# Attention and two-layer MLP on one core: early quotients through two other DMA queues, two runs of scores for the first four pairs, a later scaling, a new table of shifts

## The chip, the cores and the metric

The kernel runs on one core of a Trainium2 chip. The metric is the device time of one execution in microseconds (us), the median of several runs. A core has a TensorE (PE, with PEld for its weight loads), a VectorE (DVE), a ScalarE (ACT), a GpSimd (POOL) and a SyncE (SP). SP, ACT and POOL can each issue DMA transfers; a DMA instruction stands in the order of the engine that issues it, and whatever it has to wait for holds up what stands behind it on that engine.

## The reference, cut

```python
# q, k, v: (8, 8, 576, 64)   f: (8, 8, 576) in 0.8..1   w_in: (512, 2048)   w_out: (2048, 512)
scores = matmul(q, k.T) / 8
cum    = cumsum(log(clip(f, 1e-4, 1)))              # along the sequence
scores = where(causal, -1e9, scores + cum[:, None] - cum[None, :])
attn   = exp(scores - max);  attn = attn / (sum(attn) + 1e-9)
x      = matmul(attn, v) -> (4608, 512)             # tokens x (heads * 64)
h      = x @ w_in;  g = max(h, 0) + alpha * min(h, 0);  out = g @ w_out
```

All in float32.

## The kernel before

**The parts.** Heads go in pairs, `attention(n)` for n = 0 to 31; pairs 4b to 4b+3 make the rows of batch b. A pair has its scores in four row tiles (widths 128, 256, 384, 512) per head and one tail tile for the last 64 rows of both heads. For each tile PE multiplies q and k (L381, `bank<-rqk`), DVE adds the mask and decay `Z` and takes the row minimum in one instruction (L830, the tail at L680), ACT takes the exponential with the row sum into `st` (L637), PE transposes the tile (L651), DVE (pairs 0 to 3, even widths) or ACT copies it out of the bank (L646, L647), and PE multiplies it with v (L381, `bank<-big,vr`). ACT copies the values to `xs` (L925).

**Quotients.** When a pair has all sums, ACT adds eps (L726), DVE takes the reciprocal (L727), PE transposes the 128x9 result (L729), ACT copies it to `R` (L730), and then the row of 576 quotients per head has to reach all partitions: SP stores `R` to DRAM (L735, `rd<-R`) and SP loads it back three times, spread over 64 partitions each (`fetch`, L742, `ri<-rd`). There is one buffer `ri`. The values are multiplied with it (L939, two instructions a pair: DVE for n < 8, POOL later), and ACT and POOL split the product into the two parts that the MLP takes (L941, L943, into `xx`). Pair 3 (`hurry`) does without DRAM: `quick` spreads its quotients by PE products. From pair 6 on, two pairs share one store (`mate`), so there are five stores of 9x128 and one of 18x128 for n < 8, and seven groups of three fetches.

**Masks.** f is loaded, clipped, its logarithm taken and summed (`cu`, L403). DVE scales it by -8 (`o_8`, L408), SP stores it (`c8`, L410) and a second form of it (`c8p`), and each pair's `Z` is loaded from there, spread over partitions (L533, L575), before POOL adds the triangle (L557, L558, L577). The first pair's mask is made by PE products and DVE (L550).

**Between.** w_in comes in 16 chunks, each loaded by SP (L362) and split by DVE (L367, L368, L371, L372), ACT and POOL. The first MLP layer (`bank<-xx,wi`) starts as soon as batch 0 is there and from then on fills PE wherever attention leaves it idle; its results go to DRAM, and the second layer runs from about 500 us.

**The order.** Nothing is ordered by hand. `Plan` holds all operations with an engine, an assumed cost, the data and buffers they need, and a key; it walks through time, gives each engine the operation that can start earliest and, among these, the one with the smallest key. To the key it adds `SHIFT[(kind, pair)]`, a table of some 280 numbers (kinds are loads L, masks D and Z, scores A, transposes T, values V, quotients Q, multiplies X, splits W). Each engine then runs its instructions in the planned order. The order of scores of the first four pairs comes from `stretch`, once for each set of tiles in L953. Where the plan sees PE idle for over 0.5 us before 82 us, `fill` (L476) writes matmuls of `ident` with itself into the order; they compute nothing.

Of the kernel before, what the change touches and what calls it, by code (L numbers as in the profile page):

```python
# [13 lines left out]
AF = mybir.ActivationFunctionType  # L14
# [3 lines left out]
B, H, S, D = 8, 8, 576, 64  # L18
# [85 lines left out]
class Plan:  # L104
# [36 lines left out]
    def run(self):  # L141
# [7 lines left out]
        while left:  # L149
# [41 lines left out]
            if o.kb:  # L191
                self.chan = max(self.chan, s + 1.4) + o.kb / (220.0 if s < FAR else 280.0)
                end = self.chan + 1.0
# [29 lines left out]
def attention_moe(  # L223
# [110 lines left out]
    def c_act(n):  # L334
        return 65 + n / 1.2
# [53 lines left out]
    o_w1 = op("POOL", 100, lambda: po.memset(warm, 1.0), -102)  # L389
    o_w2 = op("ACT", 1400, lambda: ac.activation(warm, warm, AF.Ln), -102, [o_w1])  # L390
    o_f = op("SP", 500, lambda: sy.dma_start(ft(), f.rearrange("b h s -> (b h) s")), -100, (), [bft], kb=144)
    o_z = op("DVE", 500, lambda: ve.memset(z(), 0.0), -100, (), [bz])

    o_clip, o_ln, o_sc = [], [], []
    PC = ((0, 256), (256, S))
    for a0, a1 in PC:
        o_clip.append(op("DVE", 130 + (a1 - a0), lambda a0=a0, a1=a1: ve.tensor_scalar(
            ft()[:, a0:a1], ft()[:, a0:a1], 1e-4, 1.0, ALU.max, ALU.min), -100, [o_f], [bft]))
    for i, (a0, a1) in enumerate(PC):
        o_ln.append(op("ACT", c_act(a1 - a0) + 180, lambda a0=a0, a1=a1: ac.activation(ft()[:, a0:a1], ft()[:, a0:a1], AF.Ln), -100, [o_clip[i]], [bft]))  # L400
    o_warm = op("ACT", 1500, lambda: ac.activation(warm, ft()[0:1, 0:1], AF.Exp), -99, o_ln, [bft])
    for i, (a0, a1) in enumerate(PC):
        o_sc.append(op("DVE", 100 + 2.2 * (a1 - a0), lambda i=i, a0=a0, a1=a1: ve.tensor_tensor_scan(  # L403
            cu()[:, a0:a1], ft()[:, a0:a1], z()[:, a0:a1], cu()[:, a0 - 1 : a0] if i else 0.0, ALU.add, ALU.add),
            -100, [o_ln[i], o_z] + o_sc, [bft, bz, bcu]))
    o_scan = o_sc[1]

    o_8 = [op("DVE", 150 + (a1 - a0) / 1.92, lambda a0=a0, a1=a1: ve.tensor_scalar_mul(ft()[:, a0:a1], cu()[:, a0:a1], -8.0),  # L408
              -100, [o_sc[i]], [bcu, bft]) for i, (a0, a1) in enumerate(PC)]
    o_c8 = op("SP", 400, lambda: sy.dma_start(c8, ft()), -49, o_8, [bft], kb=147)  # L410
    o_c8p = [op("SP", 400, lambda k=k: sy.dma_start(c8p[:, 128 * k : 128 * k + 128].rearrange("p (s c) -> p s c", c=32),
                                                    c8[:, 0:512].rearrange("p (s k c) -> p s k c", k=4, c=32)[:, :, k]), 6, [o_c8], kb=60) for k in range(4)]
    o_c8p.append(op("SP", 400, lambda: sy.dma_start(c8p[:, 512:S], c8[:, 512:S]), 6, [o_c8], kb=16))
# [67 lines left out]
    first_up = []
    x_ops, x_late, xt_ops, s_0 = {}, [], [], []

    def load_n(n, held):

        b, p = divmod(n, NP)
        first = n == 0
        kl, kc, bh = NS * n - 16, NS * n - 7, b * H + 2 * p
        bqk, bZ = Buf(rqk), Buf(rZ)
        q_, k_ = (lambda: bqk.t[:, 0:QW]), (lambda: bqk.t[:, QW : QW + S])  # L490
        plan.at("L", n)
        kq = -99 if first else -59 if n == 1 else kl
        dq = [] if first else [o_scan]
# [23 lines left out]
        for h in range(2):  # L517
# [876 lines left out]
```

## Time and profile before

| | |
|---|---|
| median of 3 runs | 991.21 us (990.93 to 991.32) |
| the profiled execution | 990.63 us, its span 988.8 us |
| busy share of the span | PE 99%, DVE 84%, ACT 62%, POOL 38% |
| granted TensorE clock | 1.00 of full speed (2.4 GHz) in all stretches |
| first MLP product | at 59.01 us |

The span is what the trace covers; the rest of the time lies around it. A stretch is read by its busy times: an engine whose busy time is as long as the stretch sets its end. The chain of waits goes back from the last instruction, at each step to what released it. "Idle before" is the time an engine stood still just ahead of an instruction, with what it waited for.

### The profile page before, as it was taken

To read this page: it belongs to the slowest core of one execution; us is meant where nothing else is said; L and a number is where in the kernel's file an instruction comes from. 1 tells how busy PE (TensorE), PEld (TensorE's weight loads), DVE (VectorE), ACT (ScalarE), POOL (GpSimd) and SP (SyncE) were. 2 spreads that over 40 slices of the span, in tenths; PEclk is the share of its full clock that TensorE was granted. 3 is DMA by queue.
4 is the path that set the end of the run, shared out by engine and by line. 5 is a ranking of instruction groups with operands and counts; after the bars stand their busy time and mean duration, and the time that the engine had idled before them with its cause. 6 is when DMAs were issued, how large, how long until landed. Compare 5 with 4: busy or idle time off the path is not lost.

```text
span 988.8 us, 20133 instructions
## 1 busy us (share of the span) xinstructions
PE 982.2 (99%) x6935; PEld 827.5 (84%) x6935; DVE 830.7 (84%) x1585; ACT 614.4 (62%) x1399; POOL 375.5 (38%) x652
## 2 busy tenths in 40 slices
PE   9999999999999999999999999999999999999998
PEld 5777788888888888888888888999888988898898
DVE  6899988878787778779637988789999999999995
ACT  7888887878677686767635655645444543544352
POOL 5465976888868797777350000000000000000000
PEclk9999999999999999999999999999999999999999
DMA  7977768888888798796757655553444344334521
GB/s 216 260 215 259 251 217 247 254 246 262 247 251 255 224 261 249 219 267 200 215 180 237 203 172 200 174 170 107 149 128 149 107 149 155 122 107 149 169 67 43
DMA packets 133876, 191.68 MB, mean 194 GB/s; under 512 B 22647, under 2 KB 84590, under 8 KB 133774
## 3 DMA queue, kind: packets, MB, share of 16 engines
q1 hardware_dynamic: 128878, 175.73, 57.2%
q0 software_dynamic: 4608, 14.46, 5.3%
q8 instruction: 55, 0.90, 0.4%
q14 instruction: 47, 0.39, 0.1%
q10 hardware_dynamic: 288, 0.20, 0.1%
HBM read 102.95 MB, written 48.67 MB: 153 GB/s over the span
## 4 chain that ended last, share of the span: by engine, by line
PE 96%; DVE 2%; issue 1%; DMA 0%; ACT 0%; DVEq 0%; ACTq 0%
PE bank L381 93%; PE bank L651 2%; PE bank L444 0%; DMA wr<-in_w_in_dram 0%; DVE xs L939 0%; DVE hs L371 0%; DVE big L830 0%; PE bank L729 0%; PE bank L479 0%; DVE hs L1316 0%; DVE big L646 0%; DVE hs L368 0%; DVE wr L371 0%; DVE hs L367 0%; DVE wr L368 0%
## 5 line engine op out<-in xcount | busy, mean ns | idle before, releaser
L381 PE MATMUL bank<-xx,wi 128*128 128x512 f32 x1728 | 407.2, 392 | 0.0
L381 PEld LDWEIGHTS bank<-xx,wi 128*128 128x128 f32 x1728 | 320.4, 188 | 69.6 <-issue 3.0
L637 ACT ACTIVATE big<-big,st 128x384 f32<-128x384 f32 (+4 forms) x272 | 157.7, 582 | 25.8 <-DVE st L830 24.2
L1029 DVE SCALAR_TENSOR_TENSOR hs<-bank,sa,hs 128x512 f32<-128x512 f32 x116 | 86.5, 745 | 54.0 <-ACT hs L1027 52.5
L1027 ACT ACTIVATE hs<-bank,ab 128x512 f32<-128x512 f32 x116 | 79.7, 687 | 70.6 <-PE bank L381 69.0
L830 DVE CUSTOM_DVE_ANT_0 big<-bank,Z 128x384 f32<-128x384 f32 (+1 forms) x220 | 93.0, 480 | 34.2 <-PE bank L381 27.7
L1268 ACT ACTIVATE xx<-gj 128x1792 fp32r<-128x1792 f32 x37 | 62.4, 1701 | 95.0 <-DVE gj L1261 57.3
L381 PE MATMUL bank<-wot,xx 128*128 128x256 f32 (+1 forms) x734 | 120.6, 323 | 0.0
L381 PE MATMUL bank<-wi,xx 128*128 128x256 f32 (+1 forms) x734 | 120.6, 323 | 0.0
L381 PEld LDWEIGHTS bank<-wi,xx 128*128 128x128 f32 x734 | 106.8, 189 | 12.2
L381 PEld LDWEIGHTS bank<-wot,xx 128*128 128x128 f32 x734 | 106.8, 189 | 12.2
L846 DVE STREAM_TRANSPOSE big<-big 128x768 f32<-128x768 f32 x96 | 90.3, 959 | 8.5 <-ACT big L637 8.5
L543 POOL TENSOR_TENSOR Z<-Z,tri 128x128 f32<-128x128 f32 x192 | 79.8, 444 | 34.3 <-DVE Z L513 30.7
L1269 DVE TENSOR_TENSOR xx<-gj,xx 128x1792 fp32r<-128x1792 f32 x37 | 74.4, 2018 | 2.5 <-ACT xx L1268 2.5
L943 POOL TENSOR_TENSOR xx<-xs,xx 128x256 fp32r<-128x256 f32 x64 | 49.0, 781 | 43.2 <-ACT xx L941 42.7
L381 PEld LDWEIGHTS bank<-big,vr 128*64 128x64 f32 x1168 | 53.7, 137 | 9.1 <-issue 5.5
L381 PE MATMUL bank<-wi,gh 128*128 128x256 f32 (+1 forms) x370 | 60.9, 322 | 0.0
L381 PE MATMUL bank<-wot,gh 128*128 128x256 f32 (+1 forms) x370 | 60.9, 322 | 0.0
L381 PE MATMUL bank<-big,vr 128*64 128x128 f32 (+1 forms) x1168 | 59.7, 260 | 0.0
L381 PEld LDWEIGHTS bank<-wot,gh 128*128 128x128 f32 x370 | 53.9, 189 | 6.0
L381 PEld LDWEIGHTS bank<-wi,gh 128*128 128x128 f32 x370 | 53.9, 189 | 6.0
L1298 ACT ACTIVATE hs<-bank 128x256 f32<-128x256 f32 x102 | 36.5, 384 | 24.9 <-PE bank L381 24.6
(164 smaller groups left out, 1585.6 us busy)
## 6 DMA issues: line engine op xcount, KB each, us to landing
hd<-hs SPq DMA_DIRECT2D x144, 256.0 KB
gj<-hd SPq DMA_DIRECT2D x50, 512.0 KB
rqk<-in_qk_dram SPq DMA_DIRECT2D x28, 512.0 KB
wx<-hd SPq DMA_DIRECT2D x22, 512.0 KB
vr<-in_vv_dram SPq DMA_DIRECT2D x32, 320.0 KB
wr<-in_w_in_dram SPq DMA_DIRECT2D x16, 512.0 KB
wx<-in_w_out_dram SPq DMA_DIRECT2D x16, 512.0 KB
out_dram<-hs SPq DMA_DIRECT2D x30, 256.0 KB
```

The costliest lines, as they stand in the source:

```text
L381: pe.matmul(o, lhsT, rhs, start=start, stop=stop)
L543: ms.append(op("POOL", c_po(128), lambda to=to, i=i, zd=zd: po.tensor_tensor(to()[:, :, -1:], zd()[:, :, i : i + 1], tk(), ALU.add), kc + ...
L637: ex = op("ACT", c_exp(w), lambda: ac.activation(at(bt.t), at(bt.t), AF.Exp, bias=lo()[:, col : col + 1], scale=-1.0, accum_out=su()[:, co ...
L651: pe.transpose(t[:, c : c + 128], src[:, 128 * j : 128 * j + 128], ident)
L830: ve.tensor_tensor_reduce(out=o if turned else blk(o), in0=blk(bS.t[:, c0 : c0 + w]), in1=in1(), scale=-0.125, scalar=3.0e38, op0=ALU.add, ...
L846: ve.transpose(part(b_[:, 0 : 768 if k < 3 else MW]), part(bE.t[:, c0 : c0 + (768 if k < 3 else MW)]))
L943: xl = op("POOL", c_po(256), lambda r=r, t0=t0: po.tensor_tensor(bx.t[:, 1, t0 : t0 + 256], bxs[r].t[:, 0:256], bx.t[:, 0, t0 : t0 + 256]. ...
L1027: cp = op("ACT", c_act(512), lambda bh=bh, bs=bs, fc=fc: ac.activation(bs.t, bh.t, AF.Relu, scale=ab[:, fc : fc + 1]), -1000, [last, o_sg] ...
L1029: cp = op("DVE", c_dve(512), lambda bh=bh, bs=bs, fc=fc: ve.scalar_tensor_tensor(bs.t, bh.t, sa[:, fc : fc + 1], bs.t, ALU.mult, ALU.add), ...
L1268: hi = op("ACT", c_acs(896 * GW), lambda w=w, bgh=bgh: ac.activation(bgh.t[:, 0], w(), AF.Copy), key, [o2], [bj, bgh])
L1269: lo = op("DVE", c_dve(896 * GW), lambda w=w, bgh=bgh: tt(bgh.t[:, 1], w(), bgh.t[:, 0].bitcast(F32), ALU.subtract), key + 0.1, [hi], [bj, ...
L1298: side = op("ACT", c_act(256), lambda m=m, slot=slot: ac.activation(bs.t[:, slot], bo[m].t[:, 256:512], AF.Copy), kd, [last], [bo[m], bs])
```

## The change

Five edits. (1) For n < 8 the quotient store (L735) is issued by ACT and the three fetches (L742) by POOL; later pairs stay on SP. In the plan such a transfer has a fixed duration (2.6 us and its size) and no longer occupies the planned DMA channel. (2) Pairs 0 to 3 take their scores in two runs, tiles (0, 1, 3) and then tile (2), where before there were three: (0, 1), (2), (3). (3) The scaling by -8, its store and the second form are written after `attention(0)`, and the scaling waits for the first mask addition (`first_m`) too. (4) The warming Exp reads `warm` alone. (5) SHIFT has new numbers throughout. Two further lines (`short`, `k0_`) change nothing for this kernel's settings.

```diff
+NO = 8
-SHIFT = {('L', 0): 9.4, ('D', 0): 2.2, ('Z', 0): 60.6, ('A', 0): 2.2, ...
+SHIFT = {('L', 0): 101.9, ('D', 0): 18.1, ('Z', 0): 2.4, ('A', 0): 21.2, ...
@@ Plan
-            if o.kb:
+            if o.kb < 0:
+                end = s + 2.6 - o.kb / 220.0
+            elif o.kb:
@@
-    o_warm = op("ACT", 1500, lambda: ac.activation(warm, ft()[0:1, 0:1], AF.Exp), -99, o_ln, [bft])
+    o_warm = op("ACT", 1500, lambda: ac.activation(warm, warm, AF.Exp), -99, o_ln)
...
-    o_8 = [op("DVE", ..., lambda a0=a0, a1=a1: ve.tensor_scalar_mul(ft()[:, a0:a1], cu()[:, a0:a1], -8.0),
-              -100, [o_sc[i]], [bcu, bft]) for i, (a0, a1) in enumerate(PC)]
-    o_c8 = op("SP", 400, lambda: sy.dma_start(c8, ft()), -49, o_8, [bft], kb=147)
...
+                first_m.append(m1)
@@ quotients
-            st_ = op("SP", 350, lambda: sy.dma_start(d.rearrange("(c q) -> c q", q=128), bR.t[0:w]), key, [r_], [bR], kb=w / 2)
+            own = n < NO
+            q1, e1_ = (ac, "ACT") if own else (sy, "SP")
+            st_ = op(e1_, 350, lambda: q1.dma_start(d.rearrange("(c q) -> c q", q=128), bR.t[0:w]), key, [r_], [bR], kb=w / (-2 if own else 2))
@@ fetch
-                ri_ops.append(op("SP", 350, lambda ...: sy.dma_start(
+                q2, e2_ = (po, "POOL") if n < NO else (sy, "SP")
+                ri_ops.append(op(e2_, 500 if n < NO else 350, lambda ...: q2.dma_start(
...
-                    key, [st_], [bri], kb=(c1 - c0) / 4))
+                    key, [st_], [bri], kb=(c1 - c0) / (-4 if n < NO else 4)))
@@ attention
-        for tiles in ((0, 1), (2,), (3,)) if n < NE else ...
+        for tiles in ((0, 1, 3), (2,)) if n < NE else ...
@@ behind attention(0)
+    o_8 = [op("DVE", ..., -100, [o_sc[i], first_m[0]], [bcu, bft]) for i, (a0, a1) in enumerate(PC)]
+    o_c8 = op("SP", 400, lambda: sy.dma_start(c8, ft()), -49, o_8, [bft], kb=147)
...
```

What the new table does to the order is seen at four places. In the rows, `rqk_103` and `rqk_104` are the two buffers of q and k, `Z_105`/`Z_107` and `Zt_106`/`Zt_108` the masks, `st_112` to `st_114` the row sums, `xs_0`/`xs_1` the values, `ri_119` the quotients spread out; behind the change the lines stand one to three lower or higher (L940 is L939 of before, L831 is L830, L678 is L680, L644 is L646, L725 is L727, L635 is L637, L384 is L381, L476 is L479).

DVE, around the last reductions of pair 3 (512 wide) and the multiplies of pair 1, before:

```order
L830 ISA big,st_112<-bank_83,Z_107 128x384
L830 ISA big,st_112<-bank_80,Z_107 128x384
L367 TENSOR_SCALAR hs<-wr 128x512
L368 SCALAR_TENSOR_TENSOR hs<-wr,hs 128x512
L371 SCALAR_TENSOR_TENSOR hs<-wr,hs 128x512
L372 SCALAR_TENSOR_TENSOR hs<-wi,hs 128x512
L646 COPY big<-bank_81 128x4x64 x2
L830 ISA big,st_112<-bank_77,Z_107 128x512
L939 TENSOR_TENSOR xs_1_116<-xs_1_116,ri_119 128x256
L939 TENSOR_TENSOR xs_1_118<-xs_1_118,ri_119 128x320
L830 ISA big,st_112<-bank_79,Z_107 128x512
```

(rows that only read out an accumulator are left out). The same place after:

```order
L940 TENSOR_TENSOR xs_1_116<-xs_1_116,ri_119 128x256
L940 TENSOR_TENSOR xs_1_118<-xs_1_118,ri_119 128x320
L831 ISA big,st_112<-bank_80,Z_107 128x512
L831 ISA big,st_112<-bank_78,Z_107 128x512
L644 COPY big<-bank_82 128x4x128
L678 ISA big,st_112<-bank_81,Zt_108 128x256
L678 ISA big,st_112<-bank_79,Zt_108,st_112 128x320
L831 ISA big,st_112<-bank_83,Z_107 128x384
L831 ISA big,st_112<-bank_76,Z_107 128x384
L644 COPY big<-bank_77 128x4x128
L370 TENSOR_SCALAR wr<-wr 128x512
L371 SCALAR_TENSOR_TENSOR wr<-wr 128x512
```

The multiplies moved ahead of both 512-wide reductions, those stand ahead of the tail and of tile 2, and the four instructions of a w_in split (L367 to L372) went from before the 512-wide reductions to behind all of them.

DVE, from the reciprocal of pair 0 (L727 before, L725 after) to its multiplies with the quotients, before (of the stretch between, the last rows):

```order
L727 RECIPROCAL st_112<-st_112 128x9
L830 ISA wr,st_113<-bank_76,Z_107 128x128
...
L830 ISA big,st_114<-bank_78,Z_105 128x512
L830 ISA big,st_114<-bank_77,Z_105 128x512
L830 ISA big,st_112<-bank_80,Z_107 128x128
L646 COPY big<-bank_83 128x4x64 x2
L830 ISA wr,st_112<-bank_82,Z_107 128x128
L939 TENSOR_TENSOR xs_0_115<-xs_0_115,ri_119 128x256
L939 TENSOR_TENSOR xs_0_117<-xs_0_117,ri_119 128x320
```

and after:

```order
L725 RECIPROCAL st_112<-st_112 128x9
L644 COPY big<-bank_80 128x4x64
L644 COPY big<-bank_76 128x4x128
L644 COPY big<-bank_78 128x4x128
L831 ISA big,st_113<-bank_77,Z_107 128x128
L831 ISA big,st_113<-bank_81,Z_107 128x512
...
L678 ISA big,st_113<-bank_76,Zt_108,st_113 128x320
L468 TENSOR_SCALAR sg<-al 128x16
...
L831 ISA big,st_113<-bank_81,Z_107 128x384
L940 TENSOR_TENSOR xs_0_117<-xs_0_117,ri_119 128x320
L940 TENSOR_TENSOR xs_0_115<-xs_0_115,ri_119 128x256
```

Before, all reductions of pairs 1 and 2 (`st_113`, `st_114`) and the first of pair 3 stand between; after, most of those of pair 1 and four small instructions on alpha (L468 to L471).

POOL, behind the masks of pair 1 (`Z_107`, `Zt_108`), after:

```order
L555 TENSOR_TENSOR Z_107<-Z_107,tri 128x2x128
L556 TENSOR_TENSOR Z_107<-Z_107,tri 128x2x128
L575 TENSOR_TENSOR Zt_108<-Zt_108,tri_124 128x64
L743 DMA ri_119<-rd_63 64x576
L743 DMA ri_119<-rd_63 64x64
L743 DMA ri_119<-rd_63 64x512
L555 TENSOR_TENSOR Z_105<-Z_105,tri 128x2x128
L556 TENSOR_TENSOR Z_105<-Z_105,tri 128x2x128
```

The three fetches are new on POOL; before, the masks of pair 2 (`Z_105`) followed directly on those of pair 1.

SP, from the store of c8 (`c_59`) to the loads of pair 1's masks, before:

```order
L410 DMA c_59<-big 64x576
L618 DMA vr<-in_vv_dram 128x640
L467 DMA al<-in_alpha_dram 128x16
L618 DMA vr<-in_vv_dram 128x640
L533 DMA Z_107<-c_59 128x2x256 x2
L575 DMA Zt_108<-c_59 64x576 x2
```

and after:

```order
L1041 DMA c_59<-big 64x576
L616 DMA vr<-in_vv_dram 128x640
L492 DMA rqk_103<-in_qk_dram 128x640
L530 DMA Z_107<-c_59 128x2x256 x2
L573 DMA Zt_108<-c_59 64x576 x2
```

A load of pair 2's q into `rqk_103`, which pair 0 still reads, has come to stand ahead of the loads of pair 1's masks. The idents written by `fill` are 4 in the order after and 14 before (each stands for two matmuls of the trace); of every other kind there are as many instructions as before.

## Rows read from the trace of the kernel before

**Rows 1.** Page, part 1: busy us of each engine, share of the span, instructions.

```profile
PE 982.2 (99%) x6935; PEld 827.5 (84%) x6935; DVE 830.7 (84%) x1585; ACT 614.4 (62%) x1399; POOL 375.5 (38%) x652
```

**Rows 2.** Windows: us, PE, PEld, DVE, ACT, POOL busy, granted clock, DMA share, GB/s.

```profile
0.00:59.00 59.00, 56.24 (x488) 38.68 (x488) 47.89 (x147) 47.15 (x141) 30.15 (x66) 1.00 0.79 232
59.00:110.00 51.00, 50.48 (x356) 38.90 (x356) 47.21 (x103) 44.75 (x123) 39.01 (x46) 1.00 0.83 256
110.00:500.00 390.00, 390.00 (x3245) 323.59 (x3245) 309.93 (x771) 289.88 (x835) 297.13 (x527) 1.00 0.81 240
```

**Rows 3.** Lines, PE at L479: the matmuls of fill; busy us, mean ns.

```profile
L479 PE MATMUL bank<-ident 128*128 128x128 f32 x28 | 3.9, 278 | 0.0
```

**Rows 4.** Timeline of PE: start, duration, idle before in brackets with its releaser.

```profile
1.47 4.45 PE L444 MATMUL bank<-wr 128*128 128x512 bf16 x10 [1.47 <-DVE wr L441]
9.47 3.09 PE L381 MATMUL bank<-rqk 64*128 64x384 f32 x11
48.66 0.66 PE L651 MATMUL bank<-ident,big 128*128 128x128 f32 x4 [0.33 <-ACT big L637]
50.68 0.66 PE L651 MATMUL bank<-ident,big 128*128 128x128 f32 x4 [0.93 <-ACT big L637]
51.91 1.83 PE L479 MATMUL bank<-ident 128*128 128x128 f32 x14
59.01 1.66 PE L381 MATMUL bank<-xx,wi 128*128 128x512 f32 x6
```

**Rows 5.** The chain that ended last, pieces between 42 and 51 us: start, us.

```profile
42.83 0.43 DVE hs L367
43.28 1.06 DVE hs L368
44.37 1.05 DVE hs L371
49.82 0.82 ACT big L637 x2
```

**Rows 6.** Timeline of DVE from pair 1's first reduction to pair 0's multiplies.

```profile
15.52 0.28 DVE L830 CUSTOM_DVE_ANT_0 big<-bank,Z 128x128 f32<-128x128 f32 x1
17.72 0.20 DVE L727 RECIPROCAL st<-st 128x9 f32<-128x9 f32 x1
18.34 0.69 DVE L646 COPY big<-bank 128x512 f32<-128x512 f32 x1
20.84 0.17 DVE L471 TENSOR_SCALAR sg<-al 128x16 f32<-128x16 f32 x1
22.37 0.54 DVE L830 CUSTOM_DVE_ANT_0 big<-bank,Z 128x384 f32<-128x384 f32 x1
33.33 0.82 DVE L939 TENSOR_TENSOR xs<-xs,ri 128x256 f32<-128x256 f32 x2
```

**Rows 7.** Page, part 5: the reductions; busy us, mean ns of one.

```profile
L830 DVE CUSTOM_DVE_ANT_0 big<-bank,Z 128x384 f32<-128x384 f32 (+1 forms) x220 | 93.0, 480 | 34.2 <-PE bank L381 27.7
```

**Rows 8.** Timeline of SP: DMA issues; a store of quotients with its fetches.

```profile
9.16 0.90 SPq L533 DMA_DIRECT2D Z<-c  x2
193.54 0.31 SPq L735 DMA_DIRECT2D rd<-R  x1
196.15 1.77 SPq L742 DMA_DIRECT2D ri<-rd  x3
```

**Rows 9.** Line L854: POOL's issues, ns min/median/max; issue to landing.

```profile
L854 POOL DMA_DIRECT2D big<-big x72: 498/500/661, 143.3 to 486.1; - x72
DMA to landing us min/median/max: 2.1/4.0/6.0
```

**Rows 10.** Timeline of POOL: pair 1's first mask; a multiply that waited for quotients.

```profile
13.22 0.67 POOL L557 TENSOR_TENSOR Z<-Z,tri 128x256 f32<-128x256 f32 x1 [2.33 <-DMA Z<-c]
212.34 1.57 POOL L939 TENSOR_TENSOR xs<-xs,ri 128x256 f32<-128x256 f32 x2 [3.95 <-DMA ri<-rd]
```

**Rows 11.** Line L1314, DMA issues by ACT: ns min/median/max.

```profile
L1314 ACTq DMA_DIRECT2D out_dram<-hs x2: 338/359/380, 985.3 to 985.9; - x2
```

More of the change, by code (lines that the diff above doesn't have):

```diff
@@ L406, in attention_moe @@
     o_scan = o_sc[1]
-    o_8 = [op("DVE", 150 + (a1 - a0) / 1.92, lambda a0=a0, a1=a1: ve.tensor_scalar_mul(ft()[:, a0:a1], cu()[:, a0:a1], -8.0),
-              -100, [o_sc[i]], [bcu, bft]) for i, (a0, a1) in enumerate(PC)]
-    o_c8 = op("SP", 400, lambda: sy.dma_start(c8, ft()), -49, o_8, [bft], kb=147)
-    o_c8p = [op("SP", 400, lambda k=k: sy.dma_start(c8p[:, 128 * k : 128 * k + 128].rearrange("p (s c) -> p s c", c=32),
-                                                    c8[:, 0:512].rearrange("p (s k c) -> p s k c", k=4, c=32)[:, :, k]), 6, [o_c8], kb=60) for k in range(4)]
-    o_c8p.append(op("SP", 400, lambda: sy.dma_start(c8p[:, 512:S], c8[:, 512:S]), 6, [o_c8], kb=16))
     o_id = op("POOL", 600, lambda: make_identity(nc, ident), -98)
@@ L479, in fill @@
             pe.matmul(bank[:, 0:128], ident, ident, start=True, stop=True)
-    first_up = []
+    first_up, first_m = [], []
     x_ops, x_late, xt_ops, s_0 = {}, [], [], []
@@ L587, in load_n @@
                 op("POOL", c_po(128), lambda: po.tensor_copy(
-                    k0_().rearrange("p (k x) -> p k x", k=4), k_()[:, 0:512].rearrange("p (k x) -> p k x", k=4)[:, :, 0:32]), kc, l_qk, [bqk, bQ])]
+                    k0_().rearrange("p (k x) -> p k x", k=4), (k_()[:, 0:512].rearrange("p (k x) -> p k x", k=4)[:, :, 0:32] if n >= NX[0] else k_()[:, 0:128].rearrange("p (k x) -> p k x", k=4))), kc, l_qk, [bqk, bQ])]
         for hi, lo, raw, z, w, ld in ((Qh, Ql, q_, 128, QW, l_qk[:1]), (Kh, Kl, k_, 0, S, l_qk)):
@@ L741, in fetch @@
             for o, (c0, c1), s0 in ((0, (0, S), 0), (64, (512, S), S), (64, (0, 512), S + 64)):
-                ri_ops.append(op("SP", 350, lambda o=o, c0=c0, c1=c1, s0=s0: sy.dma_start(
+                q2, e2_ = (po, "POOL") if n < NO else (sy, "SP")
+                ri_ops.append(op(e2_, 500 if n < NO else 350, lambda o=o, c0=c0, c1=c1, s0=s0, q2=q2: q2.dma_start(
                     bri.t[o : o + 64, c0:c1], d[s0 : s0 + c1 - c0].rearrange("(o s) -> o s", o=1).broadcast_to([64, c1 - c0])),
-                    key, [st_], [bri], kb=(c1 - c0) / 4))
+                    key, [st_], [bri], kb=(c1 - c0) / (-4 if n < NO else 4)))
         e1, be = [None, None], [{}, {}]
@@ L752, in rows_of_scores @@
                 w = 128 * i + 128
-                short = turned and i == 0
+                short = len(terms) > 3 and i == 0
                 some = terms[3:] if short else terms[:3]
@@ L952, in attention @@
         bt = None
-        for tiles in ((0, 1), (2,), (3,)) if n < NE else ((2, 3, 0, 1),) if turned else ((0, 1, 3), (2,)):
+        for tiles in ((0, 1, 3), (2,)) if n < NE else ((2, 3, 0, 1),) if turned else ((0, 1, 3), (2,)):
             where = visit(k0) if turned else stretch(tiles, -61 if n + tiles[0] == 0 else k0 + k_[tiles[0]])
@@ L1036, in attention_moe @@
     op("-", 0, lambda: setattr(plan, "fill", fill), 0, [o_id] + first_up)
+    plan.at("", 0)
+    o_8 = [op("DVE", 150 + (a1 - a0) / 1.92, lambda a0=a0, a1=a1: ve.tensor_scalar_mul(ft()[:, a0:a1], cu()[:, a0:a1], -8.0),
+              -100, [o_sc[i], first_m[0]], [bcu, bft]) for i, (a0, a1) in enumerate(PC)]
+    o_c8 = op("SP", 400, lambda: sy.dma_start(c8, ft()), -49, o_8, [bft], kb=147)
+    o_c8p = [op("SP", 400, lambda k=k: sy.dma_start(c8p[:, 128 * k : 128 * k + 128].rearrange("p (s c) -> p s c", c=32),
+                                                    c8[:, 0:512].rearrange("p (s k c) -> p s k c", k=4, c=32)[:, :, k]), 6, [o_c8], kb=60) for k in range(4)]
+    o_c8p.append(op("SP", 400, lambda: sy.dma_start(c8p[:, 512:S], c8[:, 512:S]), 6, [o_c8], kb=16))
     o_sg = None
```

2 lines of the change are left out of this document (1 added, 1 removed).

## The prediction

> **What bounds the kernel now.** I read the page first: PE is busy for 982.2 of 988.8 us, and no other engine comes near it [rows 1]. So the question is only where the missing time lies. The windows answer it: between 110 and 500 us PE is busy for 390.00 of 390.00 us, at a granted clock of 1.00 (2.4 GHz), and between 59 and 110 us it idles for 0.52 us [rows 2]. The reason is the MLP: from its first product at 59.01 us on [rows 4], its matmuls stand ready to fill whatever attention leaves. After that moment every operation of attention that comes a little earlier or later just changes places with MLP work. What can be won or lost is thus what stands on PE before 59 us and isn't work:
>
> - the lead-in of 1.47 us [rows 4], which the change doesn't touch;
> - idle time: 59.00 - 56.24 - 1.47 = 1.29 us. Nearly all of it is two gaps, 0.33 and 0.93 us, ahead of the transposes at 48.66 and 50.68 us, which waited for ACT's exponentials [rows 4];
> - matmuls of `fill`, which count as busy and compute nothing: 28 of them [rows 3]. Their busy total is 3.9 us, 0.14 each; matmuls overlap on PE, and 14 of them in a row took 1.83 us from the first start to the last end [rows 4], so that the spacing is (1.83 - 0.28)/13 = 0.12. I take 0.12, 3.3 us in all.
>
> The chain of waits says why PE had to wait at 48 to 51 us: it goes from the exponentials of pair 3 (49.82) back to DVE, which did three instructions of a w_in split, 0.43 + 1.06 + 1.05 us, ahead of the 512-wide reductions of that pair [rows 5]. DVE and ACT are busy for 47.89 and 47.15 of the first 59 us [rows 2]: they have slack, but not much.
>
> **The change part by part**, against the profiled execution of 990.63 us, which is 0.58 us under the median of 991.21.
>
> *The table and the two runs of scores.* Matmuls of fill go from 28 to 8 (4 rows in the order, two matmuls each): 20 x 0.12 = -2.4 us, if real work or nothing takes their place. In the new order of DVE the 512-wide reductions of pair 3 stand ahead of the split, so what held up the two gaps is behind them: -1.26 us. What is late next there is tile 2 of pair 3 (384 wide), last in the new order; it is shorter by a quarter, and no split stands ahead of it. Work on PE, DVE and ACT is otherwise the same, instruction for instruction. Bounds of this part: 0 (the plan wrote fewer idents and PE idles in their place) and -3.66 us. I take the whole, less what follows.
>
> *Store by ACT, fetches by POOL.* ACT gets 6 issues of 0.36 us [rows 11], 2.2 us over the first eight pairs; POOL gets 21 of 0.50 us [rows 9], 10.5 us. POOL is busy for 30.15 of the first 59 us [rows 2], so there its issues lie in idle time; ACT has 11.9 us idle, and half its six stores fall there: 1 us, hidden by the same idle time, or up to 1 us if not. SP loses 27 issues; nothing in the chain waits for SP, so that is worth 0. The store on ACT can have to wait for an earlier transfer before it is issued, with the next pair's exponentials queued behind it; for that no row has a price, and I take 0, between 0 and one landing of 2.1 us [rows 9].
>
> What the order does change is how soon the quotients are wanted. Before, the reciprocal of pair 0 stood at 17.72 and its multiplies at 33.33 us, 15.6 us later [rows 6]. Now nine reductions at 93.0/220 = 0.42 us [rows 7], three copies of at most 0.69 and the four alpha instructions, 22.37 - 20.84 = 1.53 us [rows 6], lie between, some 6.9 us; at DVE's busy share of 0.81 [rows 2], 8.5 us. Within that time must come: eps, transpose and copy of the quotients (some 1.6 us from 17.72 to the store), the issue 0.36 [rows 11], the store's landing 2.3 (issue at 193.54, first fetch at 196.15, less the issue [rows 8]), three issues on POOL 1.5, and the last fetch's landing, 2.1, 4.0 or 6.0 us [rows 9]: 7.9, 9.8 or 11.8 us. The multiplies are in DVE's line, so reductions of pair 1 and the copies that PE waits for are queued behind them. The wait is 0, 1.3 or 3.3 us for pair 0, and about the same for pair 1, where also about 7 us of DVE work is left between. A wait of DVE is not yet one of PE: the 11.1 us that DVE stood idle in the first 59 us went with 1.29 us of idle PE. By that ratio 2 x 1.3 us would cost 0.3; if all of it came through, 2.6. I take a third, +0.9 us, and keep 0 and +6.6 as ends.
>
> *The masks of pair 1.* The loads of pair 1's masks now follow a load into the q buffer that pair 0 reads. PE's reads end at 12.56 (9.47 + 3.09 [rows 4]); before, the mask loads were issued at 9.16 [rows 8] and POOL could begin at 13.22 [rows 10], 4.1 us later. Now it is 12.56 + 0.45 + 4.1 = 17.1 us, where the first reduction of pair 1 ran at 15.52 [rows 6]. On PE the transposes, the tail and the values of pair 0 and the scores of pair 1 lie before anything that needs those reductions, so I take 0; the end is 17.1 - 15.5 = 1.6 us.
>
> *Scaling later.* DVE's scaling moves behind the first mask addition; the first reduction may come earlier by up to the 0.6 us of the scaling, but it still waits for mask additions that ACT and POOL make. 0, down to -0.3.
>
> Sum: -2.4 - 1.26 + 0.9 = -2.76: 987.87 as a run, and 988.4 on the median's level. Ends without a change of mechanism: 987.5 (no wait on quotients, the two gaps and the fills gone) and 991.2.
>
> **The rivals.**
>
> A, *PE's gaps only change their kind.* Fewer idents are written because the plan sees less idle PE, and the plan's costs are assumptions. DVE and ACT at 81% and 80% of the stretch speak for it: if they set the pace, what was an ident becomes idle time. The 28 idents stood at spots where the plan expected a gap and the trace shows none on top of them, which is for the plan. Then 0 of 3.66 is won and the small waits stay hidden: 991.2 us. With the masks' 1.6 us late on top of my sum, 988.4 + 1.6 = 990.0, the result is of the same kind.
>
> B, *slower: the multiplies wait for quotients fetched by POOL.* It is the wait above at its far end: fetches landing after 6.0 us [rows 9], 3.3 us of standing DVE for each of pairs 0 and 1. It begins to count where the last fetch takes over 2.7 us to land (8.5 - 7.9 + 2.1) and decides the sign where over half of 2 x 3.3 us comes through to PE. The trace has such a wait: POOL stood for 3.95 us in one of its multiplies for quotients [rows 10]. Against it stands POOL's steady issue, 498 to 661 ns [rows 9]. With the gain of 3.66 turned into idle time and 3.3 of 6.6 us through, 991.2 + 3.3 = 994.5 us.
> The Trainium skill ("SBUF - State Buffer", section "SBUF: two separate sides") speaks for B: a DMA issued from GpSimd has its descriptors written by GpSimd over a port pair that it shares with VectorE, so that a VectorE instruction that holds the ports can make such a transfer late. By that rule POOL is the wrong queue beside a DVE that is 81% busy; the 144 issues of L854 by POOL in this trace, at most 661 ns long, do not show it, the landing of up to 6.0 us leaves room for it.
>
> C, *slower later: the new order starves PE behind 110 us.* 390.00 of 390.00 [rows 2] leaves nothing to win and something to lose, and every number of the table is new. A wait like the 3.95 us of [rows 10] coming through once would give 988.4 + 3.95 = 992.4 us.
>
> **How the numbers follow.** My forecast has 0.52: the two places it lives on can be read in the order. A has 0.27, B 0.14, C 0.07. The measurement of this kernel can tell about 0.2%, 2 us, from no change: faster is below 989.2, slower above 993.2. Of the forecast's 0.52, spread between 987.5 and 989.8, some 0.07 lies over 989.2; of A's 0.27, 0.05 lie faster (half the gain won); B counts mostly as slower, 0.13, and C half. That makes faster 0.50, same 0.33, slower 0.17. The range reaches from 986.7 (the lower end 987.5, less the 0.52 us idle between 59 and 110 us and 0.3 of the scaling) to 993.6, which leaves out most of B and part of C.
>
> **What would show it.** Right: in the trace of the changed kernel the first MLP product near 56 us, some 8 matmuls of fill, no gap on PE ahead of pair 3's transposes; DVE's multiplies of pairs 0 and 1 with a wait of 0 to 2 us for `ri`. A: the MLP product at 59 us as before, with new PE gaps of 3 us in all ended by DVE or ACT. B: waits of over 3 us at DVE's multiplies for `ri`, and PE idle behind them; the first MLP product behind 60 us. C: windows between 110 and 500 us with PE below 100%. Masks: a wait of DVE for POOL's `Z` at about 17 us. My forecast is wrong if PE's idle time before the first MLP product isn't about 2 us smaller, fills included, or if the rest doesn't keep PE full.

## The result: slower by 1.1%, and what the profile after shows

| | before | after |
|---|---|---|
| median | 991.07 us (990.85 to 991.32, 4 runs) | 1001.84 us (1001.71 to 1002.66, 4 runs) |
| ratio, 95% interval | | 1.0109 (1.0097 to 1.0121) |
| span of the profiled execution | 988.8 us | 1000.8 us |
| first MLP product | 59.01 us | 63.99 us |
| matmuls of fill | 28 | 8 |

I had forecast 988.4 us, with 986.7 to 993.6 as the range. The kernel lost 10.8 us where I expected 2.7 to be won. In the profiled executions, whose spans lie 12.0 us apart, 5.0 us of that came before the first MLP product and the other 7.0 behind it. (In the kernel after, most lines stand one to three away from those of before; L940 multiplies the values by the quotients, L743 fetches these, L735 stores them.)

The windows of after (stretch, its us, busy us of PE, PEld, DVE, ACT, POOL, granted clock, DMA share, GB/s) answer to [rows 2]:

```profile
0.00:59.00 59.00, 50.77 (x398) 33.41 (x400) 36.85 (x134) 42.34 (x130) 31.47 (x74) 0.97 0.73 211
59.00:110.00 51.00, 50.15 (x400) 38.22 (x399) 42.66 (x103) 44.03 (x118) 32.27 (x45) 1.00 0.75 232
110.00:500.00 390.00, 386.90 (x3188) 319.74 (x3186) 312.27 (x766) 287.48 (x828) 299.89 (x534) 1.00 0.82 241
```

PE idles for 8.23 us in the first 59 where it idled for 2.76, for 0.85 up to 110 where it was 0.52, and for 3.10 between 110 and 500, where before not a hundredth was missing. DVE did 11 us less in the first 59 us. The waits of PE (timeline; the idle time stands in brackets, with what ended it) show where:

```profile
31.90 0.52 PE L649 MATMUL bank<-ident,big 128*128 128x128 f32 x3 [3.38 <-DVE st L831]
...
46.82 0.52 PE L649 MATMUL bank<-ident,big 128*128 128x128 f32 x3 [2.50 <-DVE st L831]
```

Both wait for a reduction of DVE, and DVE's timeline says what that one stood behind:

```profile
16.53 0.21 DVE L725 RECIPROCAL st<-st 128x9 f32<-128x9 f32 x1 [0.30 <-ACT st L724]
...
30.45 0.83 DVE L940 TENSOR_TENSOR xs<-xs,ri 128x320 f32<-128x320 f32 x2 [5.89 <-DMA ri<-rd]
...
32.94 0.20 DVE L725 RECIPROCAL st<-st 128x9 f32<-128x9 f32 x1
...
45.24 0.83 DVE L940 TENSOR_TENSOR xs<-xs,ri 128x256 f32<-128x256 f32 x2 [2.64 <-DMA ri<-rd]
```

The multiplies of pairs 0 and 1 wait 5.89 and 2.64 us for the quotients: rival B, at its place and with more than its price. The chain of waits (start, us, what) takes the trip of pair 0's quotients (the store to DRAM and the fetches back) apart:

```profile
12.73 0.33 SPq L492
...
13.60 0.46 SPq L530
...
14.62 5.17 DMA Zt<-c
...
19.87 4.46 DMA rd<-R
...
24.62 1.20 POOL ri L743 x2
...
25.82 4.51 DMA ri<-rd
...
30.45 0.83 DVE xs L940 x2
```

From the end: the multiply waited for a fetch that took 4.51 us to land; POOL had issued it when the store had landed, after 4.46 us; and ACT had issued the store at 19.87, though its data had been copied to `R` by 18.79 (`18.54 0.25` in ACT's timeline), because it waited for a mask load of pair 1 (`Zt`) to land, at 14.62 + 5.17 = 19.79. That load SP had issued late, behind a load that waited for PE until 12.73. So the second link of the chain is the masks. Nothing in the data ties that store to that mask: in the program the store carries, beside its wait for ACT's copy, a wait on one of the eight DMA semaphores that the transfers of SP and ACT use in turn (DMAHW5), and this one was last used by that mask load.

The clock added to it. Windows around the second gap:

```profile
44.00:46.00 2.00, 0.33 (x3) 0.00 (x0) 0.76 (x3) 0.30 (x1) 0.00 (x0) 1.00 1.03 278
46.00:48.00 2.00, 1.18 (x7) 0.94 (x8) 2.00 (x7) 1.81 (x5) 1.80 (x3) 0.85 1.10 267
48.00:50.00 2.00, 2.00 (x10) 1.29 (x10) 1.82 (x9) 1.60 (x7) 2.00 (x4) 0.50 1.08 249
50.00:52.00 2.00, 2.00 (x14) 1.13 (x14) 1.97 (x6) 2.00 (x7) 0.57 (x2) 0.79 1.07 366
```

Behind 2.50 us without work the granted clock stood at 0.50 (1.2 GHz), and PE, busy all the time from 46.82 on, did, by an estimate from these windows, 2 x (0.15 + 0.50 + 0.21) = 1.7 us less than at 2.4 GHz.

### The profile page after: what moved, and what is told of

It is laid out like the page before. It is cut to its first block, busy times and chain, and to the rows that moved or that the text cites. A ratio compares the mean times of both kernels' runs of the same rounds, so it can differ in the third digit from the quotient of the medians.

```text
span 1000.8 us, 20109 instructions
## 1 busy us (share of the span) xinstructions
PE 984.0 (98%) x6915; PEld 826.6 (83%) x6915; DVE 825.2 (82%) x1585; ACT 614.3 (61%) x1399; POOL 378.3 (38%) x673
## 3 DMA queue, kind: packets, MB, share of 16 engines
q0 software_dynamic: 5504, 16.53, 6.0%
## 4 chain that ended last, share of the span: by engine, by line
PE 88%; DMA 6%; DVE 2%; POOL 2%; issue 1%; ACT 1%; SPq 0%; DVEq 0%; POOLq 0%; ACTq 0%
PE bank L384 86%; DMA ri<-rd 1%; PE bank L649 1%; DMA hd<-hs 1%; DMA rd<-R 1%; DMA vr<-in_vv_dram 1%; DMA Z<-c8p 1%; POOL Z L540 1%; DMA rqk<-in_qk_dram 1%; DMA Zt<-c 1%; PE bank L441 0%; POOL wi L380 0%; DVE xs L940 0%; POOL ri L743 0%; DVE big L831 0%
## 5 line engine op out<-in xcount | busy, mean ns | idle before, releaser
L384 PE MATMUL bank<-xx,wi 128*128 128x512 f32 x1728 | 406.7, 392 | 1.0 <-DVE st L831 1.0
L384 PEld LDWEIGHTS bank<-xx,wi 128*128 128x128 f32 x1728 | 320.5, 188 | 69.4 <-issue 2.4
L635 ACT ACTIVATE big<-big,st 128x384 f32<-128x384 f32 (+4 forms) x272 | 157.6, 582 | 25.0 <-DVE st L831 24.5
L831 DVE CUSTOM_DVE_ANT_0 big<-bank,Z 128x384 f32<-128x384 f32 (+1 forms) x220 | 93.1, 480 | 36.6 <-PE bank L384 29.4
L384 PE MATMUL bank<-wi,xx 128*128 128x256 f32 (+1 forms) x734 | 120.6, 323 | 0.0
L384 PE MATMUL bank<-wot,xx 128*128 128x256 f32 (+1 forms) x734 | 120.6, 323 | 0.0
L384 PEld LDWEIGHTS bank<-wi,xx 128*128 128x128 f32 x734 | 106.8, 189 | 12.2
L384 PEld LDWEIGHTS bank<-wot,xx 128*128 128x128 f32 x734 | 106.8, 189 | 12.2
L384 PEld LDWEIGHTS bank<-big,vr 128*64 128x64 f32 x1168 | 53.7, 137 | 9.7 <-issue 4.3
L384 PE MATMUL bank<-wi,gh 128*128 128x256 f32 (+1 forms) x370 | 60.9, 322 | 0.0
L384 PE MATMUL bank<-wot,gh 128*128 128x256 f32 (+1 forms) x370 | 60.9, 322 | 0.0
L384 PE MATMUL bank<-big,vr 128*64 128x128 f32 (+1 forms) x1168 | 59.7, 260 | 0.2 <-DVE st L831 0.2
L384 PEld LDWEIGHTS bank<-wot,gh 128*128 128x128 f32 x370 | 53.9, 189 | 6.0
L384 PEld LDWEIGHTS bank<-wi,gh 128*128 128x128 f32 x370 | 53.8, 189 | 6.0
```

The lines of the kernel that those rows point to most:

```text
L384: pe.matmul(o, lhsT, rhs, start=start, stop=stop)
L635: ex = op("ACT", c_exp(w), lambda: ac.activation(at(bt.t), at(bt.t), AF.Exp, bias=lo()[:, col : col + 1], scale=-1.0, accum_out=su()[:, co ...
L831: ve.tensor_tensor_reduce(out=o if turned else blk(o), in0=blk(bS.t[:, c0 : c0 + w]), in1=in1(), scale=-0.125, scalar=3.0e38, op0=ALU.add, ...
```

## The experiments

Times are medians beside the median of before on the same chip, 990.8 to 991.0 us throughout. Two kinds of kernels were run: those that keep the planned order of PE, DVE, ACT and POOL and move only a transfer, and those that let the plan draw everything anew.

### Which queue carries the quotients (order kept)

```diff
# a_all_sp: in the kernel after
-lambda: q1.dma_start(d..., bR.t[0:w])            # store
+lambda: sy.dma_start(d..., bR.t[0:w])
-lambda ..., q2=q2: q2.dma_start(bri.t[...], ...)  # fetch
+lambda ..., q2=q2: sy.dma_start(bri.t[...], ...)
# a_store_sp: the first of the two alone
```

> The changed kernel (1001.84 us), with every engine's order as it is, only the quotient stores and fetches of the first eight pairs are issued by SP, at the place in its line that the plan gives them by time. Theory Q, the queues of ACT and POOL are what makes the trip through DRAM late: DVE's waits for ri at its multiplies (5.89 and 2.64 us in the changed kernel) shrink below 2 us in sum and the time falls to 991 to 994 us. Theory O, the new order asks for the quotients too early whatever queue brings them: the waits stay at 5 us or more in sum and the time stays over 997 us.

> The changed kernel with only the stores issued by SP, the fetches still by POOL, the order as it is. If the wait of ACT's first store for a mask load's landing (it stood until 19.81 us, while its data were there at about 18.2) is a main cause, the multiply of pair 0 comes 1.5 us or more earlier than at 30.45 us and the time falls by 1.5 us or more. If SP has the store no earlier (its own line is full of mask loads then), under 0.5 us.

Measured: both on SP 997.78 us (996.66 to 1000.0, ratio 1.0064, 1.0045 to 1.0083), the store alone 1001.57 (1.0061 to 1.0127). The multiply of pair 0 with both on SP:

```profile
30.25 0.83 DVE L940 TENSOR_TENSOR xs<-xs,ri 128x320 f32<-128x320 f32 x2 [5.09 <-DMA ri<-rd]
...
44.50 0.82 DVE L940 TENSOR_TENSOR xs<-xs,ri 128x256 f32<-128x256 f32 x2
```

By its numbers Theory O came out, at its very edge (5.09 us of waits, 997.78 us). But neither theory holds as I put it: pair 1's wait went (2.64 to 0), and pair 0's stayed. SP was issuing masks and copies of c8 until 21.85 us, and the store, next in its line, then waited until 22.25 for its semaphore in turn, last used by a mask load of pair 2 that landed at 22.19. The store by SP alone is worth nothing that its spread shows (999.17 to 1003.58). So some 4 us hang on POOL as the queue of the fetches once the store is on SP; the fetches on SP with the store left on ACT were not run. The 5 us wait of pair 0 has another cause, in line with the chain above. The clock hides part of the gain: behind that wait it stood at 0.50, 0.50 and 0.61 from 32 to 38 us (lines in the last section), which is by the same estimate 2.8 us of PE's work, more than the 1.7 of the kernel after.

The other way round, in the kernel before:

```diff
-st_ = op("SP", 350, lambda: sy.dma_start(d..., bR.t[0:w]), ...
+st_ = op("SP", 350, lambda: (ac if n < NN else sy).dma_start(d..., bR.t[0:w]), ...
-lambda ...: sy.dma_start(bri.t[...], ...)
+lambda ...: (po if n < NN else sy).dma_start(bri.t[...], ...)
```

> The kernel before with its own plan and order, only that the quotient stores of the first eight pairs are issued by ACT and the fetches by POOL. Theory Q: it is slower by 3 us or more, 994 us and over. Theory O: before leaves 15.6 us between reciprocal and multiply, so a trip of some 13 us stays hidden, 991 us, at most 1 us off.

996.40 us (994.85 to 998.34; 1.0036 to 1.0065): the queues alone cost 5.4 us, with the order of before. For pairs 0 and 1 it is as Theory O has it: pair 0's multiply waits for 1.53 us, and the first MLP product stays at 58.98 us. The loss comes later. PE stands for over 2 us at two places, where it stood for 0.52 us and not at all before:

```profile
110.71 0.81 PE L381 MATMUL bank<-rqk 128*128 128x320 f32 x2 [2.09 <-DVE st L830]
...
151.19 0.58 PE L381 MATMUL bank<-Kh,Qh 128*128 128x256 f32 x1 [2.41 <-DVE st L830]
```

The second stands behind the multiplies of pairs 6 and 7, whose fetches moved to POOL too:

```profile
141.85 0.83 DVE L939 TENSOR_TENSOR xs<-xs,ri 128x256 f32<-128x256 f32 x2 [2.24 <-DMA ri<-rd]
...
149.75 0.83 DVE L939 TENSOR_TENSOR xs<-xs,ri 128x256 f32<-128x256 f32 x2 [2.82 <-DMA ri<-rd]
```

The first of these pairs' fetches was issued at 132.60 us by SP in the kernel before and at 137.15 by POOL here, behind POOL's own work. An in-order engine that is busy with masks and splits is a late queue. The first has no quotient in it. DVE came late to its reduction mainly because one instruction of a w_in split, some 10 us ahead of it, took 4.63 us, where it took 0.69 before:

```profile
98.34 4.63 DVE L368 SCALAR_TENSOR_TENSOR hs<-wr,hs 128x512 uint32<-128x512 uint32 x1
```

POOL worked beside it without a pause in both kernels, here shifted by the fetches in its line; that the shift held DVE up is not shown.

### Taking the wait away (order kept)

```diff
# a_nowait: n < 2; a_nowait8: n < 8
-d[s0 : s0 + c1 - c0].rearrange("(o s) -> o s", o=1).broadcast_to([64, c1 - c0])
+(c8[n : n + 1, 0 : c1 - c0] if n < 2 else d[...].rearrange(...)).broadcast_to([64, c1 - c0])
```

> The changed kernel, its order as it is, but for pairs 0 and 1 the fetches read a row of c8 that has long been stored (so these pairs' quotients are not the right ones), so that the multiplies do not wait for the store. If the quotients' trip is the cause of all of the 10.8 us, the time falls to about 990 us. If the stalls of the changed kernel behind 85 us (some 6 us, at 86, 118, 130, 147 and 294 us) have causes of their own, it stays at 995 to 997 us. If the masks of pair 1, late, take its place, over 998 us.

> As the run before it (a_nowait, 996.54 us), but now the fetches of all pairs below 8 read a row of c8 instead of the stored quotients (their quotients are not the right ones), so that no multiply of the first eight pairs waits for a store. Theory T, the trip of the quotients through DRAM, in a tight order, is all of the loss: the remaining stalls at 80, 124 and 140 us go too and the time is 990 us or less. Theory N, the new table loses time behind 75 us by other waits (mask and q loads, w_in splits): still 994 us or more.

996.54 us (994.15 to 999.50) and 998.28 (995.14 to 999.32). The first MLP product comes at 57.2 and 57.5 us, 1.5 to 1.8 earlier than before, so the first stage moves the way I forecast once no quotient's store holds it up, by about half as much (I had said near 56). Yet the whole is 5.5 to 7.5 us slower than before, so Theory T is out as the whole cause: 3.6 to 5.3 us of the 10.8 hang on the wait for the store, the rest lies elsewhere. Some of the rest can still be the fetches by POOL, which stay in these kernels: in a_nowait8 the multiplies of pairs 1, 6 and 7 wait 1.16, 1.71 and 1.35 us for them. Part of it is PE idling behind 59 us again, 0.66 us up to 110 and 2.39 up to 200 in a_nowait. No single wait there would explain the loss; the longest of PE is 0.87 us.

### The masks of pair 1 (order kept but for one step of SP)

```diff
# order of SP; Plan.run holds back one operation by four of SP's
 c_59<-big                  # store of c8
 vr<-in_vv_dram
-rqk_103<-in_qk_dram        # q of pair 2
 Z_107<-c_59 x2             # masks of pair 1
 Zt_108<-c_59 x2
+rqk_103<-in_qk_dram
```

> The changed kernel, all engines' orders kept but for one step on SP: the load of pair 2's q, which waits for PE's last read of pair 0, is issued behind the loads of pair 1's masks and not ahead of them. In the changed kernel the mask loads were issued at 13.16 us, and ACT's store of pair 0's quotients waited until 19.81 us for one of them to land. If that chain carries the loss of pair 0, the masks come at some 9 us, the store at about 18.3, the multiply some 1.5 us earlier, and the time falls by 1 to 3 us. If the store's landing and the fetch are what count, under 0.5 us.

999.22 us (996.42 to 1002.66; 1.0066 to 1.0107): 2.6 us less than after by the medians, but with an interval that overlaps that of after (1.0097 to 1.0121), so alone it is a weak sign. The multiply of pair 0 comes at 29.03 instead of 30.45 us, pair 1's wait falls from 2.64 to 0.91. But not by the link that I named. The chain of this run:

```profile
14.30 5.22 DMA Z<-c
...
19.60 2.82 DMA rd<-R
...
22.71 1.20 POOL ri L754 x2
23.91 5.00 DMA ri<-rd
...
29.03 0.83 DVE xs L951 x2
```

The store still leaves at 19.60 (0.27 us earlier), now waiting for a mask load of pair 2, the last user of the semaphore whose turn it is. What got shorter is its landing, 2.82 us instead of 4.46. That the mask loads beside it had slowed it is my reading; no run shows it by itself.

```diff
# a_masks_sp: a_masks_first and a_all_sp together
```

> The changed kernel, orders kept, with both moves on SP at once: pair 1's masks loaded ahead of pair 2's q (alone 999.22 us) and the quotient stores and fetches issued by SP (alone 997.78, against 1001.84 of the changed kernel). If the two causes are separate, the gains of 2.6 and 4.1 us add: about 995 us. If they are the same wait seen twice, 997 us or more.

994.28 us (992.32 to 997.40; ratio 1.0038, 1.0028 to 1.0049). 2.6 + 4.1 = 6.7 was forecast, 7.6 measured, and one wait seen twice would have left 997 us or more: so there are two causes. How exactly they add can't be told, since each of these three kernels has a spread of over 3 us and the lower clock of a_all_sp (some 2.8 us) is gone here. Beside a_all_sp the masks are worth 3.5 us (997.78 to 994.28), the clearest sign that they count. The wait of pair 0 falls to 3.56 us, the first MLP product stands at 58.39 us. With not one instruction of PE, DVE, ACT or POOL in another order (POOL and ACT only lose their DMAs), 7.6 of the 10.8 us are back. That is the largest share that any run settles. Of the 3.4 us that remain, the profile shows 1.88 us, PE's idle time behind 110 us. The profiled execution took 992.32 us, the fastest of the ten, so it does not show the rest:

```profile
0.00:59.00 59.00, 54.06 (x471) 36.64 (x472) 42.06 (x149) 47.23 (x145) 29.38 (x68) 1.00 0.75 222
59.00:110.00 51.00, 51.00 (x361) 39.22 (x359) 47.12 (x99) 45.19 (x122) 35.38 (x42) 1.00 0.81 259
110.00:500.00 390.00, 388.12 (x3224) 321.38 (x3224) 311.61 (x773) 288.58 (x829) 293.91 (x527) 1.00 0.81 240
```

### The idents

```diff
# b_nofill: in the kernel before
-FILL = 82.0
+FILL = 0.0
```

> The kernel before without the idents of fill (28 matmuls on PE, 3.3 us by my count), nothing else. My sum took each ident as 0.12 us lost: then 988 us. If the idents stand where PE would idle anyway, the time stays at 991 us, and 2.4 us of the forecast's gain were never there. If the granted clock falls in the stretches where PE now idles (it stood at 0.50 to 0.85 between 46 and 52 us in the changed kernel, behind 2.5 us without work), the kernel gets slower, 991.5 to 994 us.

991.62 us (990.94 to 993.01, 11 runs; ratio 0.9998 to 1.0016). Taking all 28 away gains nothing; the first MLP product comes at 58.66 us, 0.35 earlier, and even that is not in the time. Before and without, the timeline of PE where six of them stood:

```profile
45.53 0.83 PE L479 MATMUL bank<-ident 128*128 128x128 f32 x6
46.29 2.04 PE L381 MATMUL bank<-rqk 64*128 64x128 f32 x12
48.66 0.66 PE L651 MATMUL bank<-ident,big 128*128 128x128 f32 x4 [0.33 <-ACT big L637]
```

```profile
45.73 2.69 PE L381 MATMUL bank<-rqk 64*128 64x128 f32 x12
48.75 0.66 PE L651 MATMUL bank<-ident,big 128*128 128x128 f32 x4 [0.33 <-ACT big L637]
...
52.72 0.28 PE L729 MATMUL bank<-ident,st 128*9 128x128 f32 x1 [0.75 <-DVE st L727]
```

The twelve score matmuls take 2.69 us instead of 2.04 and end where they ended (48.42 and 48.33 us): something later than the idents sets their end, and what they stand is booked as busy. At the place of the 14 idents 0.75 us of idle time now shows, ended by DVE. The granted clock stays at 1.00 in this run: behind the lead-in PE's gaps are at most 0.93 us up to 109 us.

### Each edit alone, and each undone (the plan draws the order anew)

```diff
# a_lat5: after, the plan's constant         # b_scale: before with edit 3 alone
-end = s + 2.6 - o.kb / 220.0                # b_newtab: before with the new table alone
+end = s + 5.0 - o.kb / 220.0                # b_2runs: before with edit 2 alone
# a_no0: after with NO = 0                   # a_early: after without edit 3
# a_oldtab: after with the old table         # a_3runs: after without edit 2
```

> The changed kernel with one constant of the plan changed: a transfer of quotients is planned at 5.0 us and its size, not 2.6, about what the trace shows (4.46 for the store of pair 0, 4.51 and 5.49 for the fetches), so that the plan itself puts the multiplies later. If the plan's belief is what placed the multiplies too early, DVE's waits for ri fall under 3 us in sum for pairs 0 and 1 and the time falls by 3 us or more, to under 999 us. If the table of shifts, made for another plan, is what matters, any time from 992 to 1010 us, with waits of another kind.

> The changed kernel with NO = 0: the plan itself puts stores and fetches of quotients on SP, as in the kernel before; new table, two runs of scores and later scaling stay. If the queues are the change's loss, 991 to 994 us. If the new table and the tile sets lose time by themselves, over 996 us.

> The changed kernel with the table of shifts of the kernel before, all other edits kept. If the new table is the loss, 991 to 995 us. If the queues and the plan's 2.6 us are, 996 us and over, with waits of DVE for ri.

> The kernel before with the third edit alone: the scaling by -8, its store and the second form written after attention(0), behind the first mask addition; old table, old queues. By its own size, 0.6 us of DVE at 6 us, it is worth under 0.5 us: 990.5 to 991.5. If a table of shifts fits only the code that it was made with, the plan is drawn anew by it and the time goes up by 2 us or more.

> The kernel before with the new table alone; old queues, tile sets and scaling. If the new table is good by itself and the queues lose, 988 to 991 us. If it fits only the changed code, 995 us and over.

> The changed kernel with the third edit undone: the scaling stands before the masks again, as before; queues, tile sets and new table stay, and the plan is drawn anew. If the later scaling is what put the mask loads behind the q load, they are issued at 9 us again and the time falls to 995 to 999 us. If drawing the plan anew costs more than that, 1000 us and over.

> The changed kernel with the second edit undone: three runs of scores for the first four pairs. If the two runs are a gain by themselves (pair 3's 512-wide reductions ahead of the tail), it is slower than 1001.84 by 1 us or more; if they bunch DVE's work so that the quotients are wanted too early, it is faster by 2 us or more.

> The kernel before with the second edit alone: two runs of scores, old table and queues. By my forecast's view a gain of up to 1.26 us, 990 us. If every edit that draws the plan anew under a table made for another plan costs some 5 us, as the later scaling did alone (996.97), 995 us and over.

| edit | alone in before (991) | undone in after (1001.84) |
|---|---|---|
| queues | 996.40 (b_queues, order kept) | 998.45 (a_no0) |
| two runs of scores | 1010.76 (b_2runs) | 1028.47 (a_3runs) |
| later scaling | 996.97 (b_scale) | 1012.94 (a_early) |
| new table | 993.58 (b_newtab) | 1009.09 (a_oldtab) |
| plan told of 5.0 us | | 1001.64 (a_lat5) |

The edits do not add: each of the four makes the kernel before slower alone, and undoing three of them in the kernel after makes that slower too, by 7 to 27 us. Except for b_queues, each of these draws the order of all engines anew under a table that was not made for it; I take that to be the reason, and no run separates it from what the edits do by themselves. (The warming Exp, edit 4, was not run alone.) What such a drawing costs has many forms. In b_2runs the first MLP product comes at 56.3 us, earlier than in any other run, and the kernel loses it all behind 110 us, where PE idles for 15.36 of 390 us:

```profile
151.48 1.19 PE L381 MATMUL bank<-xx,wi 128*128 128x512 f32 x2 [8.52 <-DVE st L830]
...
155.20 4.99 PE L381 MATMUL bank<-xx,wi 128*128 128x512 f32 x14 [2.52 <-POOL wi L377]
```

Only two rows speak for an edit by itself, each for its own kernel. The new table in the old code costs 2.6 us, so alone it does not cost 10.8. And undoing the queues in the kernel after gains 3.4 us. Telling the plan the true length of the trip gained nothing in sum: the waits at pairs 0 and 1 fell from 5.89 and 2.64 us to 0 and 1.34, and other waits came, one of PE of 4.04 us at 156 us; which of them belong to the table can't be told from one run. In b_scale SP has the same wrong turn as the kernel after, the load of pair 2's q ahead of pair 1's masks:

```profile
12.33 0.33 SPq L489 DMA_DIRECT2D rqk<-in_qk_dram  x1
12.76 0.90 SPq L527 DMA_DIRECT2D Z<-c  x2
```

So it is the later scaling, whose store becomes ready later in the plan, that lets this load pass the masks; no number of the table was needed for it. With that edit undone in the kernel after (a_early) the masks are issued at 8.96 us again, ahead of the q load at 12.70; that kernel then loses elsewhere.

## Why the prediction was wrong, step by step

**What bounds the kernel**: right that PE is the bound and that PE idle counts; wrong that only what stands before the first MLP product can be won or lost. This step failed by the most. I took it that the MLP's products would always be there to fill gaps, and read off a kernel in which they were. In a_nowait, a_nowait8, a_masks_sp, b_scale and b_2runs the first MLP product comes earlier than before (56.3 to 58.4 us), and each of them is slower than before, by 3.4 to 20 us. Between 110 and 500 us PE idles for 3.10 us in the kernel after and for 1.88 with masks and queues set right; in the kernel before it did not. Rival C had this, at 0.07 and 992.4 us. No rival alone came near 1001.84; the farthest was B, at 994.5.

**The idents, -2.4 us**: the first term of the sum, and it was worth nothing. I counted an ident as lost time because its record is busy time and no gap stood beside it. It had taken the place of a gap: without all 28 the time is 991.62, not 988. Rival A named this; the rows could have said so, since the plan writes an ident only where it expects PE to wait.

**The two gaps, -1.26 us**: those of pair 3 did go in the kernel after, and the first stage without the quotients' wait ended 1.5 to 1.8 us earlier (a_nowait, a_nowait8). The direction holds; the size was never seen in the time, since whatever the stage gained was lost behind 59 us.

**The quotients, +0.9 us**: right in place and mechanism, mis-sized mainly in three terms. The trip took 13.9 us for pair 0 (16.53 to 30.45) against my 7.9 to 11.8: from the store's issue to its landing it was 4.46 us where I had 0.36 + 2.3, the 2.3 from a store at 193 us, in another stage; the last fetch took 4.51 us (5.49 for pair 1) where I took 4.0; and the store waited 1.1 us on ACT (18.79 to 19.87), which I had put at 0 between 0 and 2.1. The work of DVE left in between was 24.56 - 16.53 = 8.0 us, near my 8.5. And of 8.53 us that DVE stood, 3.38 + 2.50 = 5.88 came through to PE, 0.69, not a third: DVE's slack was spread over the stage, the wait came in one piece. On top came 1.7 us at the lower clock, for which I had no term.

**The sign of B**: it had the mechanism, at 0.14, and 994.5 us for it, 7.3 less than measured. I kept it small because POOL's issues had been steady. They still are; the fetches that POOL issued in the kernel after (L743 up to 150 us; ns, min/median/max) and their landings:

```profile
L743 POOL DMA_DIRECT2D ri<-rd x21: 516/523/689, 24.6 to 148.7; - x21
...
DMA to landing us min/median/max: 2.9/4.9/6.2
```

The rule of the Trainium skill that I weighed ("SBUF - State Buffer", section "SBUF: two separate sides": descriptors written by GpSimd wait while VectorE holds the shared ports) would make these transfers land late; the landing of 4.9 us in the middle is above the 4.0 of [rows 9], and of the 15 fetches up to 110 us it is 5.3. In the kernel after DVE stood idle through the fetch of pair 0 (24.56 to 30.45), so it held no port, and that fetch still took 4.51 us (the same one issued by SP in a_all_sp took 3.39, among other transfers). At this place the rule is not the cause; no run isolates it elsewhere.

**The masks of pair 1**: I forecast 17.1 us for POOL's first mask of pair 1, the trace has 16.99. Who waits for the masks was right as well: DVE stood for 0.24 us at 19.27 for POOL's addition. The price of 0 was wrong all the same: I looked only at who waits for the masks, and not at what else waits for, or shares the DMA engines with, transfers that were all moved 4 us later. With the masks back ahead of the load the kernel gained 2.6 us by the medians, and 3.5 with stores and fetches on SP.

**The fit of table and code**: missing altogether. I priced edits one by one against rows of before, while the change replaces the order of the whole program. The runs with one edit alone span 993.58 to 1010.76 us.

What stays open: 3.4 us of the 10.8. They are there when masks and queues are set right with the new order kept; 1.88 us of PE idle behind 110 us are seen of them, and no run takes them apart.

## What to carry to other kernels

A filler instruction is time only if something real would run in its place: take the fillers out before counting them as a gain. When a transfer moves to another engine's queue, price the whole trip under the traffic of the stage where it runs, with what stands ahead of it in that engine's line and the semaphore it has to wait for, and compare that with the work left until its consumer. An order that was drawn as a whole is a whole: an edit that draws it anew has to be judged by the new order's waits, at every stage, not by the size of the edit.

## What the runs showed of the hardware

The granted clock does not follow the length of a gap alone. In the kernel after PE stood 3.38 us before 31.90 and the clock stayed at 1.00; in a_all_sp it stood 3.33 us before 31.70 and the clock fell. After, then a_all_sp:

```profile
30.00:32.00 2.00, 0.10 (x1) 0.13 (x2) 1.55 (x5) 0.96 (x3) 0.53 (x1) 1.00 0.07 16
32.00:34.00 2.00, 2.00 (x11) 1.23 (x12) 2.00 (x8) 1.61 (x6) 0.89 (x2) 1.00 0.55 130
```

```profile
30.00:32.00 2.00, 0.29 (x2) 0.33 (x3) 1.75 (x6) 1.16 (x3) 0.72 (x2) 0.69 0.68 241
32.00:34.00 2.00, 2.00 (x9) 1.68 (x8) 2.00 (x9) 1.25 (x5) 0.70 (x2) 0.50 0.62 149
34.00:36.00 2.00, 2.00 (x11) 1.06 (x11) 1.45 (x9) 1.65 (x7) 1.20 (x2) 0.50 0.89 259
36.00:38.00 2.00, 2.00 (x26) 2.00 (x25) 1.27 (x6) 2.00 (x7) 1.66 (x4) 0.61 0.05 12
```
